# Chunked attention and token-mixing MLP in one kernel: holding back the input loads so that only about three are unfinished, with w_out in four transfers

## Chip, core, metric

The kernel runs on one core of one Trainium2 chip. The metric is the device time of one execution in microseconds (us), median of several runs. Most runs of a kernel agree closely, but some are slower whatever the kernel does; for this program on one core a run is called slow when it is over 1.5% above the fastest of its kernel.

## The reference

Inputs q, k and v are 8 batches x 8 heads x 576 positions x 64 in float32, 9.4 MB each. Attention works inside chunks of 64 positions; its output, regrouped to x of 8 x 576 x 512, goes through a mixing layer.

```python
# attention, per chunk of 64 positions
scores = scale * (q_c @ k_c.T);  attn = softmax(scores);  out = attn @ v_c
# mixing, per batch; x is the attention output, 576 x 512
wq, wk = x @ w_q, x @ w_k                 # 576 x 64 each
W_tok = scale_moe * wq @ wk.T
out = relu(W_tok @ x) @ w_out             # 576 x 512, float32
```

## The kernel before

All inputs of the core are 29.6 MB and the output is 9.4 MB. The loads convert float32 to float16 on the way, and are all issued by GpSimd, in program order. This is the part that the change touches (cuts are marked):

```python
def load_qk(b, part):               # q and k of batch b; part 0: 6 of 9 slices, part 1: 3
    a, e = TR[b][part]              # (in batch 0 it is 3 and 6)
    for src, dst in ((q, qn), (k, kn)):
        for u in range(2):          # two halves of the partitions
            nc.gpsimd.dma_start(dst[b][part][CH*u : CH*u+CH, 0 : e-a, :], src[b]. ...)

def load_v(b):                      # four loads of 144 KB (written)
    for n in range(0, NP, NP // 2):
        for u in range(2):
            nc.gpsimd.dma_start(vt[b % VB][...], v[b]. ...)

def load(b):
    load_qk(b, 0)
    load_v(b)
    if b == 1:
        nc.gpsimd.dma_start(wout[:], moe_w_out.rearrange("(i p) m -> p i m", p=P))
    load_qk(b, 1)
```

Loads of batches 0 to 3 are issued at the start; those of batch b+4 after the last attention unit of batch b, in program order. There are eight completion semaphores for these loads, used in turn, so that a load waits for the load eight before it: up to eight are unfinished at a time.

What uses the loads: VectorE transposes q and k of a batch as they come (`kT`, `qT`), TensorE forms the scores from them, and a fixed plan (`PLAN`) sets the order in which the units of several batches go to TensorE.

The softmax here doesn't subtract the row's maximum and nothing guards it: scores larger than these inputs give would overflow.

Of the kernel before, what the change touches and what calls it, by code (L numbers as in the profile page):

```python
# [34 lines left out]
def kernel(  # L35
# [10 lines left out]
    nc = tc.nc  # L46
    B, H, S, D = q.shape
    DM = moe_w_out.shape[0]
    DH = moe_w_q.shape[1]
    P = 128  # L50
# [6 lines left out]
    NI = DM // P  # L57
    HS = S // 2
    W = 2 * D + 2
    WS = 172  # L60
    VB = 4
    scale_attn = 1.0 / math.sqrt(D)
    scale_moe = 1.0 / math.sqrt(DH)
    TS = 3
# [6 lines left out]
    def each(n, shape, dt, name):  # L71
        return [sb.tile(shape, dt, name=f"{name}{i}") for i in range(n)]
# [8 lines left out]
    ]  # L81
    vt = each(VB, [P, NP, W], F16, "vt")
    wqk = sb.tile([P, NI, 2 * DH], F16, name="wqk")
    wout = sb.tile([P, NI, DM], F16, name="wout")
# [18 lines left out]

    of = out.rearrange("b s m -> (b s) m")

    def load_qk(b, part):
        a, e = TR[b][part]
        for src, dst in ((q, qn), (k, kn)):
            for u in range(2):
                nc.gpsimd.dma_start(  # L110
                    dst[b][part][CH * u : CH * u + CH, 0 : e - a, :],
                    src[b]
                    .rearrange("h s d -> (h s) d")
                    .rearrange("(u t p r) d -> u p t (r d)", u=2, t=NT, r=R)[u][:, a:e, :],
                )

    def load_v(b):
        for n in range(0, NP, NP // 2):
            for u in range(2):
                nc.gpsimd.dma_start(  # L120
                    vt[b % VB][CH * u : CH * u + CH, n : n + NP // 2, D * u : D * u + D],
                    v[b]
                    .rearrange("h s d -> (h s) d")
                    .rearrange("(u g p) d -> u p g d", u=2, p=CH)[u][:, n : n + NP // 2, :],
                )

    def clear_v(i, on_scalar):
        for h in range(2):
            o = vt[i][CH * h : CH * h + CH]
            z = D - D * h  # L130
            if on_scalar:
                nc.scalar.copy(
                    o.bitcast(F32)[:, :, z // 2 : z // 2 + D // 2],
                    zero.bitcast(F32)[CH * h : CH * h + CH, None, 0 : D // 2].broadcast_to(
                        [CH, NP, D // 2]
                    ),
                )
            else:
                nc.vector.memset(o[:, :, z : z + D], 0.0)
            nc.vector.memset(o[:, :, 2 * D + h], 1.0)  # L140
            nc.vector.memset(o[:, :, 2 * D + 1 - h], 0.0)

    def load(b):
        load_qk(b, 0)
        load_v(b)
        if b == 1:
            nc.gpsimd.dma_start(wout[:], moe_w_out.rearrange("(i p) m -> p i m", p=P))
        load_qk(b, 1)

    nc.vector.memset(zero[:], 0.0)  # L150
    for i in range(VB):
        clear_v(i, i > 1)
    load(0)
    make_identity(nc, ident[:])
    for w, o in ((moe_w_q, 0), (moe_w_k, DH)):
        nc.gpsimd.dma_start(wqk[:, :, o : o + DH], w.rearrange("(i p) j -> p i j", p=P))  # L156
    for b in range(1, VB):
        load(b)

# [57 lines left out]
    def attend(b, h, a):  # L217
        af = a.rearrange("p i c -> p (i c)")
        for c in range(2 * NJ):
            m = NCH * h + c  # L220
            if c < NCH:
                t, x = m // 4, m % 4
                lhsT = est[b % 2][t // TS][:, x // 2, 2 * (t % TS) + x % 2, :]
                rhs = vt[b % VB][:, m, :]
            else:
# [94 lines left out]
    def outp(a):  # L320
# [17 lines left out]
        held.append((of[n * P : n * P + P, :], os_))  # L338
        if done.get(B - 1 - VB) == 4:
            flush()  # L340
# [3 lines left out]
    def flush():  # L344
        if "gate" not in done:
            done["gate"] = 1
            nc.sync.dma_start(mark[:], kn[B - 1][1][0:1, 0, 0:2])
        for dst, src in held:
            nc.sync.dma_start(dst, src)
        held.clear()  # L350
# [4 lines left out]
    for u in PLAN.split():  # L355
        u, _, slot = u.partition(":")
        if u[0] == "T":
            tr(int(u[3]), u[1:3])
            continue
        a = ring[int(slot)]  # L360
        if u == "F":
            fill(a, 1)
        elif u == "O":
            outp(a)
        elif len(u) == 2:
            unit[u[0]](int(u[1]), a)
        else:
            b = int(u[2])
            unit[u[0]](b, int(u[1]), a)
            if u[0] == "A":  # L370
                done[b] = done.get(b, 0) + 1
                if done[b] == 4 and b + VB < B:
                    load(b + VB)
                    if b + VB == B - 1:
                        flush()
# [30 lines left out]
```

## Time and profile before

| | before |
|---|---|
| time, median of 3 runs (4 with the run beside the result: 126.16) | 126.52 us |
| span of the profiled run | 122.5 us |
| TensorE busy | 101.7 us (83%) |
| last load lands | 90.9 us |
| last TensorE instruction ends / last store packet | 118.7 / 121.0 us |

The landing of a load is the moment when the last of 16 DMA engines has raised the load's semaphore; I read it from the semaphore events of the trace, and where I quote landings of single loads, they come from there.

From the page of the kernel before: the busy tenths of TensorE and of the DMA engines in 40 slices of the span, what the DMA engines moved in each slice (bytes written), and the line of the queue that GpSimd issues to (packets, MB, time of its packets as a share of 16 engines' span).

```profile
PE   6912246497679996999999999999999999999970
DMA  1999999999999999999999999999938999994974
GB/s 10 125 142 176 183 195 168 168 200 191 176 164 168 174 160 177 199 162 176 179 176 155 191 184 159 189 191 164 168 48 314 361 375 366 383 386 146 335 277 165
q0 software_dynamic: 58416, 14.82, 128.0%
```

TensorE has holes up to slice 15 (counted from 0; it ends at 49 us) and is then full. Loads run at about 175 GB/s (written; twice that is read) until slice 28, then the stores, mostly at 310 to 386 GB/s. The queue's share is over 100% because several packets of one engine overlap.

Windows view of the kernel before: stretch, its length, then busy us and count for TensorE, its weight loads, VectorE, ScalarE and GpSimd, the granted TensorE clock, the DMA share and GB/s.

```profile
10.00:20.00 10.00, 4.60 (x182) 4.10 (x184) 5.92 (x9) 2.32 (x3) 9.93 (x15) 0.50 1.62 185
30.00:40.00 10.00, 7.39 (x226) 5.62 (x227) 8.41 (x14) 6.74 (x11) 8.26 (x13) 1.00 1.81 171
50.00:90.00 40.00, 39.87 (x856) 25.79 (x854) 34.30 (x54) 29.45 (x49) 31.24 (x44) 0.96 1.84 174
```

From 50 to 90 us TensorE is busy 39.87 of 40 us.

Timeline of VectorE in the kernel before (start, duration, instruction, idle time before it and what ended it):

```profile
13.13 0.98 DVE L179 STREAM_TRANSPOSE qT<-qn 128x768 f32<-128x768 f32 x1 [2.22 <-DMA qn<-in_q_dram]
18.02 0.98 DVE L179 STREAM_TRANSPOSE qT<-qn 128x768 f32<-128x768 f32 x1 [1.34 <-DMA qn<-in_q_dram]
94.42 0.57 DVE L179 STREAM_TRANSPOSE qT<-qn 128x384 f32<-128x384 f32 x1
```

The first two start 0.1 us after their load has landed (13.03, 17.93). The third, of the last batch, has no wait in front: its load had landed 4.6 us earlier, at 89.8 us. By then the loads lead.

The load issues, from the DMA view of the kernel before (KB are bytes written; the last number is the median time from issue to landing):

```profile
vt<-in_v_dram POOLq DMA_DIRECT2D x32, 144.0 KB, 6.4
qn<-in_q_dram POOLq DMA_DIRECT2D x16, 192.0 KB, 5.4
kn<-in_k_dram POOLq DMA_DIRECT2D x16, 192.0 KB, 5.7
qn<-in_q_dram POOLq DMA_DIRECT2D x16, 96.0 KB, 6.0
kn<-in_k_dram POOLq DMA_DIRECT2D x16, 96.0 KB, 5.6
```

A load takes 5.4 to 6.4 us, yet one of 192 KB lands every 1.0 us: most of its time it stands in the queue.

### The profile page before, as it was taken

What the parts mean: (1) busy time and instruction counts of PE and PEld (TensorE: products, weight loads), DVE (VectorE), ACT (ScalarE), POOL (GpSimd) and SP (SyncE); (2) the same over time, 40 slices, a digit from 0 to 9 for tenths busy, and PEclk for the clock granted to TensorE, in tenths of its full rate; (3) what the DMA queues carried; (4) which work ended last, traced back from release to release, by engine and by line L of the source; (5) the groups of instructions that cost most, each with busy time, mean ns of one, the idle gap of its engine ahead of it and who ended that gap; (6) DMA issues with size and microseconds to landing.
All of it is one profiled execution on the core that took longest, in us unless ns stands there. A gap on an engine that the chain in (4) does not pass through costs nothing.

```text
span 122.5 us, 4768 instructions
## 1 busy us (share of the span) xinstructions
PE 101.7 (83%) x2039; PEld 64.4 (53%) x2039; DVE 82.9 (68%) x146; ACT 76.4 (62%) x121; POOL 71.2 (58%) x105
## 2 busy tenths in 40 slices
PE   6912246497679996999999999999999999999970
PEld 2302145394566644375776575676649667543320
DVE  5765658738896994749997789997998987210000
ACT  7921122042459784558687878678786776899960
POOL 6999997348958985996995798789100000000000
PEclk9995555557999999589999999999999999999998
DMA  1999999999999999999999999999938999994974
GB/s 10 125 142 176 183 195 168 168 200 191 176 164 168 174 160 177 199 162 176 179 176 155 191 184 159 189 191 164 168 48 314 361 375 366 383 386 146 335 277 165
DMA packets 63626, 24.57 MB, mean 201 GB/s; under 512 B 40052, under 2 KB 58996, under 8 KB 63604
## 3 DMA queue, kind: packets, MB, share of 16 engines
q0 software_dynamic: 58416, 14.82, 128.0%
q1 hardware_dynamic: 5188, 9.44, 20.7%
q8 instruction: 16, 0.26, 0.9%
q14 instruction: 6, 0.05, 0.1%
HBM read 29.62 MB, written 9.44 MB: 319 GB/s over the span
## 4 chain that ended last, share of the span: by engine, by line
PE 59%; POOL 15%; DMA 14%; issue 4%; DVE 4%; ACT 2%; DVEq 0%; ACTq 0%; POOLq 0%
PE ring L325 26%; DMA wout<-in_moe_w_out_dram 8%; PE ring L203 7%; PE ring L228 7%; POOL vt L120 6%; PE ring L260 6%; DMA vt<-in_v_dram 5%; PE ring L250 5%; POOL kn L110 4%; PE ring L305 4%; POOL qn L110 3%; PE ring L291 3%; DVE xt L255 2%; POOL wqk L156 1%; PE ring L276 1%
## 5 line engine op out<-in xcount | busy, mean ns | idle before, releaser
L325 PE MATMUL ring<-wout,rmx 128*128 128x512 f16 x144 | 35.8, 387 | 0.1
L210 ACT ACTIVATE est<-ring 128x768 f16<-128x768 f32 x24 | 18.9, 810 | 22.1 <-PE ring L203 21.7
L203 PE MATMUL ring<-qT,kT 32*64 32x64 f16 x1152 | 16.9, 214 | 13.4 <-DVE kT L179 7.6
L120 POOL DMA_DIRECT2D vt<-in_v_dram x32 | 27.3, 876 | 0.8 <-PE ring L325 0.5
L238 DVE TENSOR_TENSOR xn<-ring,rec 128x640 f16<-128x640 f32 x32 | 26.4, 824 | 1.1
L110 POOL DMA_DIRECT2D qn<-in_q_dram x32 | 21.2, 677 | 8.4 <-DMA vt<-in_v_dram 7.6
L110 POOL DMA_DIRECT2D kn<-in_k_dram x32 | 20.7, 654 | 5.5 <-DMA vt<-in_v_dram 3.4
L203 PEld LDWEIGHTS <-kT 32*64 32x64 f16 x1152 | 14.1, 118 | 17.4 <-DVE kT L179 8.4
L313 ACT ACTIVATE rmx<-ring 128x576 f16<-128x576 f32 x32 | 19.3, 652 | 3.2 <-PE ring L305 3.0
L325 PEld LDWEIGHTS <-rmx 128*128 128x128 f16 x144 | 13.1, 99 | 14.3 <-issue 2.0
L179 DVE STREAM_TRANSPOSE kT<-kn 128x384 f32<-128x384 f32 (+1 forms) x16 | 19.5, 1221 | 0.6 <-DMA kn<-in_k_dram 0.4
L255 DVE COPY xt<-ring 128x1280 f16<-128x1280 f16 x16 | 12.9, 816 | 6.5 <-PE ring L250 5.4
L228 PE MATMUL ring<-vt,est 128*64 128x130 f16 x288 | 14.8, 240 | 1.2 <-ACT est L210 1.2
L179 DVE STREAM_TRANSPOSE qT<-qn 128x384 f32<-128x384 f32 (+1 forms) x16 | 12.2, 764 | 3.8 <-DMA qn<-in_q_dram 3.8
L228 PEld LDWEIGHTS <-est 128*64 128x64 f16 x288 | 11.1, 119 | 4.9 <-issue 1.9
L250 PE MATMUL ring<-ident,xn 128*128 128x128 f16 x160 | 12.7, 237 | 0.1
L250 PEld LDWEIGHTS <-xn 128*128 128x128 f16 x160 | 10.4, 107 | 2.5 <-issue 1.3
L337 ACT COPY qn<-ring 128x512 f32<-128x512 f32 x16 | 9.4, 588 | 3.3 <-PE ring L325 3.0
L337 ACT COPY kn<-ring 128x512 f32<-128x512 f32 x16 | 9.4, 589 | 2.0 <-PE ring L325 1.9
L237 DVE RECIPROCAL rec<-ring 128x10 f32<-128x10 f32 x32 | 6.6, 207 | 4.7 <-PE ring L228 4.6
L260 PE MATMUL ring<-xt,wqk 128*128 128x288 f16 x64 | 9.6, 295 | 0.1
L267 ACT CAST wT<-ring 128x576 f16<-128x576 f32 x8 | 5.1, 639 | 7.2 <-PE ring L260 7.2
(35 smaller groups left out, 86.2 us busy)
## 6 DMA issues: line engine op xcount, KB each, us to landing
vt<-in_v_dram POOLq DMA_DIRECT2D x32, 144.0 KB, 6.4
out_dram<-qn SPq DMA_DIRECT2D x16, 256.0 KB, 3.6
out_dram<-kn SPq DMA_DIRECT2D x16, 256.0 KB, 3.6
qn<-in_q_dram POOLq DMA_DIRECT2D x16, 192.0 KB, 5.4
kn<-in_k_dram POOLq DMA_DIRECT2D x16, 192.0 KB, 5.7
qn<-in_q_dram POOLq DMA_DIRECT2D x16, 96.0 KB, 6.0
kn<-in_k_dram POOLq DMA_DIRECT2D x16, 96.0 KB, 5.6
out_dram<-spare SPq DMA_DIRECT2D x4, 256.0 KB, 2.0
```

What stands on the lines that cost most here:

```text
L110: nc.gpsimd.dma_start(dst[b][part][CH * u : CH * u + CH, 0 : e - a, :], src[b] .rearrange("h s d -> (h s) d") .rearrange("(u t p r) d -> u ...
L120: nc.gpsimd.dma_start(vt[b % VB][CH * u : CH * u + CH, n : n + NP // 2, D * u : D * u + D], v[b] .rearrange("h s d -> (h s) d") .rearrange ...
L179: nc.vector.transpose(out=o, in_=src[b][part].bitcast(F32)[:, 0 : e - a, :].rearrange("p t (r d) -> p t r d", d=32),)
L203: nc.tensor.matmul(a[CH * u : CH * u + CH, i, o : o + CH], lhsT=k_of(b, TS * s + t, 2 * u + i, ch, e), rhs=q_of(b, TS * s + t, 2 * u + i, ...
L210: nc.scalar.activation(est[b % 2][s].rearrange("p i t c -> p i (t c)"), a[:, :, 0 : 2 * TS * CH], AF.Exp, scale=scale_attn,)
L228: nc.tensor.matmul(af[CH * (c % 2) : CH * (c % 2) + CH, o : o + W], lhsT=lhsT, rhs=rhs, start=True, stop=True,)
L238: nc.vector.tensor_tensor(out=xn[b % 2] .rearrange("p j (u h d) -> p j u h d", u=2, d=D)[:, :, :, h, :], in0=xv[:, :, 0 : 2 * D].rearrange ...
L250: nc.tensor.transpose(tx[:, i, j * P : j * P + P], xn[b % 2][:, j, (2 * i + n) * P : (2 * i + n) * P + P], ident[:],)
L260: nc.tensor.matmul(a[:, h, 0:HS], lhsT=wqk[:, i, :], rhs=xt[b % 2][i % 2][:, i // 2, h * HS : h * HS + HS], start=(i == 0), stop=(i == NI ...
L313: nc.scalar.activation(rmx[(b // 2) % 2].rearrange("p (h i) n -> p i h n", h=2)[:, i, :, o : o + HS], a[:, :, 0:HS], AF.Relu, scale=scale_moe,
L325: nc.tensor.matmul(a[:, 0, :], lhsT=rmx[pr % 2][:, i, tl * P : tl * P + P], rhs=wout[:, i, :], start=(i == 0), stop=(i == NI - 1),)
L337: nc.scalar.copy(os_, a[:, 0, :])
```

## The change

Its intent: keep only a short queue, so that loads are issued close to when they can run. Each load gets an estimated transfer time in us (1.0 for 192 KB of q or k and for a v load, 0.5 for 96 KB), and waits for the most recent earlier load that has more than 2.5 us of loads behind it, itself counted. For loads of 1.0 that is the third before it. w_out comes in four transfers.

```diff
+    AHEAD = 2.5
+    queue = []
+    def fetch(dst, src, us):
+        ins = nc.gpsimd.dma_start(dst, src).ins
+        ahead = 0.0
+        for name, u in reversed(queue):
+            if ahead + u > AHEAD:
+                tc.add_manual_dep(ins, name, ..., reason="pace")   # wait for its landing
+                break
+            ahead += u
+        queue.append((ins.name, us))
     # load_qk, load_v and the weights: nc.gpsimd.dma_start(...) -> fetch(..., us)
-            nc.gpsimd.dma_start(wout[:], moe_w_out.rearrange("(i p) m -> p i m", p=P))
+            for i in range(NI):
+                fetch(wout[:, i, :], moe_w_out[i * P : i * P + P, :], 0.7)
```

No instruction of TensorE, VectorE or ScalarE changes or moves.

More of the change, by code (lines that the diff above doesn't have):

```diff
@@ L104 @@
     of = out.rearrange("b s m -> (b s) m")
+    queue = []
[4 more added lines that the diff above has]
+            if ahead + u > AHEAD:
+                tc.add_manual_dep(
+                    ins,
+                    name,
+                    mybir.DependencyInfo(mybir.DependencyClass.Sync, mybir.DependencyReason.DATA),
+                    reason="pace",
+                )
+                break
+            ahead += u
+        queue.append((ins.name, us))
     def load_qk(b, part):
@@ L109, in load_qk @@
             for u in range(2):
-                nc.gpsimd.dma_start(
+                fetch(
                     dst[b][part][CH * u : CH * u + CH, 0 : e - a, :],
@@ L114, in load_qk @@
                     .rearrange("(u t p r) d -> u p t (r d)", u=2, t=NT, r=R)[u][:, a:e, :],
+                    (e - a) / 6,
                 )
@@ L119, in load_v @@
             for u in range(2):
-                nc.gpsimd.dma_start(
+                fetch(
                     vt[b % VB][CH * u : CH * u + CH, n : n + NP // 2, D * u : D * u + D],
@@ L124, in load_v @@
                     .rearrange("(u g p) d -> u p g d", u=2, p=CH)[u][:, n : n + NP // 2, :],
+                    1.0,
                 )
@@ L155 @@
     for w, o in ((moe_w_q, 0), (moe_w_k, DH)):
-        nc.gpsimd.dma_start(wqk[:, :, o : o + DH], w.rearrange("(i p) j -> p i j", p=P))
+        fetch(wqk[:, :, o : o + DH], w.rearrange("(i p) j -> p i j", p=P), 0.5)
     for b in range(1, VB):
```

## The prediction

> **What bounds the kernel now.** Span of the profile 122.5 us, timed median 126.52.
> (1) Until about 44 us the kernel follows its loads. In the timeline the VectorE transposes of q and k start 0.1 us after their load landed (Tk03 44.08 after 43.99). TensorE is busy 46%, 70% and 74% in 10-20, 20-30 and 30-40 us.
> (2) From about 50 to 100 us TensorE is full (99% and more, windows view), and the loads are ahead: the transposes start 3 to 5 us after landing; the last 4.6 (q) and 5.7 us (k).
> (3) The last load lands at 90.9 us; stores and the TensorE tail follow.
> The DMA engines limit the loads: one of 192 KB lands every 1.0 us, of 96 KB every 0.5 us, a v load of 144 KB every 1.1 us. Eight loads are unfinished at a time (eight semaphores in turn), so a load takes 5 to 6 us from issue to landing, mostly queued.
>
> **What the change does.** No compute instruction moves. GpSimd waits before nearly each load for one about three units back (about six for the small ones). w_out in four adds three issues of 0.75 us. Fewer unfinished loads can't bring an early load forward, since the queue drains nearly in order; they can only let it run dry.
>
> **Cost.** After a landing, GpSimd starts the waiting issue 0.28 us later (20.97 to 21.25), spends 0.65 us (q, k) or 0.87 us (v) on it, and the first packets come about 0.7 us after that (first load: issue ends 2.01, packets from 2.71). That is 1.6 to 1.9 us without new work, while two loads remain: at most 2.0 us, less 0.36 us between last packet and semaphore. So the slowest DMA engine is just not fed. The Trainium skill, page "DMA: Bandwidth & Descriptors", section "Anatomy of one DMA", puts the fixed part of a transfer at about 2.0 us; the trace agrees: 2.77 us for the first load, 0.5 us of it transfer.
> Second cost: every 5 to 6 us a 16 KB instruction fetch occupies a DMA engine for 0.9 to 1.4 us (queue 8). Today the other engines run ahead (the 16 parts of a load land up to 2.3 us apart), and the queue hides it. With three loads it can't: I expect each fetch to stop the stream for some 0.5 us.
> Estimate from a hand model of the queue with these durations: loads 4 to 7 us later at 44 us, the last one 8 to 18 us later (at 99 to 109 us).
>
> **How much counts.** The delay at 44 us is nearly all critical; later delays count beyond the 4.6 us lead. So 4 to 12 us; I take 5.5 us, below the middle, since a depth of 2.5 looks chosen by trial.
>
> **Predicted: 132.0 us, 8 in 10 between 126.0 and 140.0.** Faster by over 2%: 0.08. Within 2%: 0.25. Slower by over 2%: 0.67.
>
> **What would show it.** Last load landing at 97 us or later; median from issue to landing falling from 5.5-6.4 to about 3-4 us; DMA row with 7s and 8s instead of 9s before that; GpSimd's waits on DMA rising from 13 us to over 25; TensorE idle in 50-90 us; transposes 0.1 us behind landings after 50 us.
>
> **What would make it wrong.** Descriptors started before the issue ends (a gap under 1.6 us); or deep queues slowing the stream by themselves, for instance the slow engine catching up when the others idle; then it stays within 2%.

## More of the kernel before

The output tiles are held in the old q and k tiles and are stored only when the last load has landed:

```python
def flush():
    if "gate" not in done:
        done["gate"] = 1
        nc.sync.dma_start(mark[:], kn[B - 1][1][0:1, 0, 0:2])   # waits for the last load
    for dst, src in held:
        nc.sync.dma_start(dst, src)
    held.clear()
```

## The result

| | before | after |
|---|---|---|
| time, median of 4 runs | 126.16 us | 160.28 us |
| ratio of fast runs | | 1.282 (1.268 to 1.296) |
| span of the profiled run | 122.5 | 158.6 |
| last load lands | 90.9 | 129.1 |
| last TensorE instruction ends | 118.7 | 151.7 |
| last store packet | 121.0 | 157.2 |

A ratio is the mean time of one kernel's fast runs over that of the other's of the same rounds, so it is not quite the ratio of the medians. The kernel became 28% slower, far outside the predicted range.

The same lines of the changed kernel's page:

```profile
PE   6611261940578893969797692999393969999920
DMA  3999999999999899999999996999999939999994
GB/s 39 133 102 148 121 135 78 112 130 118 144 93 123 100 144 118 131 137 124 102 120 154 109 123 65 155 115 129 139 115 74 136 59 370 352 382 376 339 381 172
q0 software_dynamic: 58464, 14.82, 99.0%
```

TensorE now has holes to the end of the loads, in slice 32. The DMA row still shows mostly 9, but the bytes tell: 65 to 155 GB/s in place of 155 to 200 (from slice 3 on). The queue's share times the span is 0.99 x 158.6 = 157 us after and 1.28 x 122.5 = 157 us before: all packets together take as long as they did. The DMA engines are not slower, they have less to do at a time.

Windows view of the changed kernel:

```profile
10.00:20.00 10.00, 2.57 (x142) 2.20 (x146) 4.34 (x6) 1.03 (x2) 5.97 (x10) 0.58 1.31 134
30.00:40.00 10.00, 3.84 (x68) 3.09 (x70) 4.39 (x8) 1.27 (x2) 6.12 (x10) 0.67 0.96 118
50.00:90.00 40.00, 32.22 (x636) 20.04 (x633) 24.23 (x38) 24.16 (x40) 22.51 (x33) 0.96 1.28 126
```

From 50 to 90 us the load stream fell from 174 to 126 GB/s and TensorE from 39.9 to 32.2 us of work.

Timeline of VectorE in the changed kernel, late in the run:

```profile
101.64 0.98 DVE L200 STREAM_TRANSPOSE qT<-qn 128x768 f32<-128x768 f32 x1 [1.59 <-DMA qn<-in_q_dram]
113.20 0.85 DVE L200 STREAM_TRANSPOSE kT<-kn 128x384 f32<-128x384 f32 x1 [2.79 <-DMA kn<-in_k_dram]
```

These loads landed at 101.55 and 113.11 us: the transposes follow them by 0.1 us again, as 15 of the 22 after 50 us do. The lead of the loads is gone, and the whole kernel runs at the pace of its loads. The waits view of the changed kernel (engine, line, whom it waited for: us in total, times, longest) says the same for VectorE, and shows that GpSimd now stands still between issues:

```profile
DVE kT L200 <- DMA kn<-in_k_dram: 22.1, 13, 3.4
DVE qT L200 <- DMA qn<-in_q_dram: 22.0, 9, 4.4
POOL kn L110 <- DMA qn<-in_q_dram: 11.1, 8, 1.9
```

GpSimd's waits on DMA add up to 12.7 us before and about 42 us after. The load issues of the changed kernel:

```profile
vt<-in_v_dram POOLq DMA_DIRECT2D x32, 144.0 KB, 4.1
qn<-in_q_dram POOLq DMA_DIRECT2D x16, 192.0 KB, 3.9
kn<-in_k_dram POOLq DMA_DIRECT2D x16, 192.0 KB, 4.3
qn<-in_q_dram POOLq DMA_DIRECT2D x16, 96.0 KB, 3.7
kn<-in_k_dram POOLq DMA_DIRECT2D x16, 96.0 KB, 3.5
```

Each load is faster by itself, about 4 us in place of 6, and the stream of them is slower by 42% (129.1 over 90.9). How both can be true is what the experiments are about.

### The profile page after: what moved, and what is told of

It is laid out like the page before. It is cut to its first block, busy times and chain, and to the rows that moved or that the text cites. A ratio compares the mean times of both kernels' runs of the same rounds, so it can differ in the third digit from the quotient of the medians.

```text
span 158.6 us, 4786 instructions
## 1 busy us (share of the span) xinstructions
PE 106.4 (67%) x2039; PEld 67.5 (43%) x2039; DVE 82.3 (52%) x146; ACT 76.7 (48%) x121; POOL 72.6 (46%) x108
## 4 chain that ended last, share of the span: by engine, by line
DMA 55%; PE 20%; issue 9%; POOL 8%; DVE 3%; ACT 0%; DVEq 0%; POOLq 0%
DMA vt<-in_v_dram 25%; DMA qn<-in_q_dram 14%; DMA kn<-in_k_dram 13%; PE ring L346 12%; POOL vt L110 3%; POOL qn L110 3%; DMA wout<-in_moe_w_out_dram 3%; POOL kn L110 2%; PE ring L249 2%; PE ring L281 2%; DVE xt L276 2%; PE ring L312 1%; PE ring L326 1%; PE ring L224 1%; DVE xn L259 1%
## 5 line engine op out<-in xcount | busy, mean ns | idle before, releaser
L224 PEld LDWEIGHTS <-kT 32*64 32x64 f16 x1152 | 14.7, 124 | 37.5 <-DVE kT L200 15.8
L346 PEld LDWEIGHTS <-rmx 128*128 128x128 f16 x144 | 13.2, 100 | 16.5 <-issue 4.5
L249 PE MATMUL ring<-vt,est 128*64 128x130 f16 x288 | 15.9, 250 | 3.6 <-DVE xt L276 2.4
L249 PEld LDWEIGHTS <-est 128*64 128x64 f16 x288 | 12.0, 126 | 7.4 <-issue 4.8
L271 PE MATMUL ring<-ident,xn 128*128 128x128 f16 x160 | 13.7, 249 | 0.5 <-DVE xn L259 0.4
L271 PEld LDWEIGHTS <-xn 128*128 128x128 f16 x160 | 11.4, 113 | 2.7 <-issue 1.1
L281 PE MATMUL ring<-xt,wqk 128*128 128x288 f16 x64 | 10.1, 306 | 0.1
L312 PE MATMUL ring<-xn,wkn 128*64 128x256 f16 x80 | 6.4, 293 | 5.1 <-DVE wkn L304 5.1
```

Of the source, the lines that this page charges most:

```text
L224: nc.tensor.matmul(a[CH * u : CH * u + CH, i, o : o + CH], lhsT=k_of(b, TS * s + t, 2 * u + i, ch, e), rhs=q_of(b, TS * s + t, 2 * u + i, ...
L249: nc.tensor.matmul(af[CH * (c % 2) : CH * (c % 2) + CH, o : o + W], lhsT=lhsT, rhs=rhs, start=True, stop=True,)
L271: nc.tensor.transpose(tx[:, i, j * P : j * P + P], xn[b % 2][:, j, (2 * i + n) * P : (2 * i + n) * P + P], ident[:],)
L281: nc.tensor.matmul(a[:, h, 0:HS], lhsT=wqk[:, i, :], rhs=xt[b % 2][i % 2][:, i // 2, h * HS : h * HS + HS], start=(i == 0), stop=(i == NI ...
L346: nc.tensor.matmul(a[:, 0, :], lhsT=rmx[pr % 2][:, i, tl * P : tl * P + P], rhs=wout[:, i, :], start=(i == 0), stop=(i == NI - 1),)
```

## The experiments

The theory (A): a load has a round trip, from the landing that lets it go to its own landing, that is longer than the work which the few other loads leave, so the DMA engines run dry. Rivals: the four w_out transfers (B); deep queues disturb, so a short one should make loads fast (C); contention with compute or with instruction fetches (D, with E as its opposite); the added waits themselves (F); the number of loads rather than the amount of work (G).

### w_out in four, no pacing

```diff
-            nc.gpsimd.dma_start(wout[:], moe_w_out.rearrange("(i p) m -> p i m", p=P))
+            for i in range(NI):
+                nc.gpsimd.dma_start(wout[:, i, :], moe_w_out[i * P : i * P + P, :])
```

> The kernel before with w_out in four transfers and no pacing. Theory A (the pacing alone costs the time): the median within 1% of before, last load landing at 90 to 92 us. Rival B (the four w_out transfers and their extra issues delay what follows): some us slower, with the landings after w_out later by that much.

Measured: median 127.45 us (before beside it: 125.33), but three of four runs were slow ones. The fast one took 125.13 us, within the 123.87 to 125.69 us of the fast runs of before. The kernel was run again:

> The kernel before with w_out in four again, since three of its four runs were slow ones: within 1% of the kernel before in fast runs.

Measured: median 128.21 us (before: 125.80); again one fast run in six, 124.37 us, within 124.04 to 125.80. So fast runs agree with the kernel before. Even the medians of all runs differ by 2.1 and 2.4 us only, of the 34, so the pacing costs the rest. Both profiles fell in slow runs (last landings at 94.0 and 92.8 us, above the 90 to 92 expected). But the run without compute and without pacing, below, has w_out in four too and lands its last load at 90.7 us, as the kernel before does (90.9). Rival B falls.

### One load at a time

```diff
-    AHEAD = 2.5
+    AHEAD = 0.0
```

> The changed kernel with the pacing depth set from 2.5 to 0: each load waits for the one before it. It measures the whole round trip of one load: the time from landing to landing. Theory A (a round trip of fixed part plus transfer: 0.28 us wake, 0.65 or 0.85 us issue, 1.2 to 1.7 us until data flow, 0.36 us to the semaphore, and 0.5 or 1.0 us transfer): 192 KB loads every 3.7 to 4.0 us, 96 KB every 3.2 to 3.5, v every 3.8 to 4.2; last landing at 370 to 410 us. Rival C (loads slow down only because deep queues of the other engines disturb them): periods near 2.5 us and the last landing near 250 us.

Measured, in one run: 386.18 us, last landing at 356.9. The DMA view of this run:

```profile
vt<-in_v_dram POOLq DMA_DIRECT2D x32, 144.0 KB, 3.5
qn<-in_q_dram POOLq DMA_DIRECT2D x16, 192.0 KB, 3.5
kn<-in_k_dram POOLq DMA_DIRECT2D x16, 192.0 KB, 3.5
qn<-in_q_dram POOLq DMA_DIRECT2D x16, 96.0 KB, 2.6
```

The queue is empty whenever a load is issued here, so these times contain no queueing: 3.5 us of the 3.9 to 4.3 us under pacing are there with nobody in front. From the events of the trace, means over each kind, in us:

| load | landing to issue | issue | to the first packet | first of 16 parts lands | last part lands | landing to landing | in the full queue of before |
|---|---|---|---|---|---|---|---|
| 96 KB q, k | 0.28 | 0.63 | 0.70 | 1.63 | 1.98 | 2.89 | 0.5 |
| 192 KB q, k | 0.35 | 0.66 | 0.70 | 2.35 | 2.81 | 3.82 | 1.0 |
| 144 KB v | 0.37 | 0.84 | 0.70 | 2.16 | 2.65 | 3.86 | 1.1 |

(The three columns after the issue count from its end.) A line through the q and k loads, 2.89 and 3.82 us, gives 1.96 us fixed and 0.93 us per 96 KB. The page "DMA: Bandwidth & Descriptors" of the Trainium skill, section "Anatomy of one DMA — SWDGE (gpsimd) path", gives about 2.0 us for the fixed part, and this is near it: 1.96 us with the 0.28 us of waking in it, 1.68 without. The slope does not agree with the full queue: there 96 KB cost 0.5 us.

A load that meets an empty queue moves its bytes at about half the rate of the stream on average. The packets of the 32 lone 192 KB loads show when: 11 to 17 start per tenth of a us for the first 0.8 us, then up to 38, the rate of the full stream. Single packets take as long as before (median 60 ns for those of 512 bytes in both runs), so it is fewer at a time. Why the start is slow these runs do not show. The same page, section "Measured (HBM→SBUF, 128 partitions, SWDGE, issued from GpSimd)", lists 138 GB/s for 64 KB and 341 GB/s for 1 MB, the same tendency (for 128 partitions; the loads here write 64); here 192 KB in the 1.56 us from the first packet (0.70) to the landing of the median part (2.62) less 0.36 us for the semaphore are some 126 GB/s, written.

Theory C falls: a lone load is no faster. Its transfer is slower. The expectation of theory A held for 192 KB and for v (3.82 and 3.86 us), but not for 96 KB (2.89 in place of 3.2 to 3.5) nor for the last landing (356.9 in place of 370 to 410): the fixed part is smaller, and the part that goes with the bytes larger, than in that sum.

### The loads without compute

The matmuls, transposes and evictions are cut, and the stores write what was loaded, so the result is wrong:

```diff
-    for u in PLAN.split():
-        ...
+    for b in range(VB, B):
+        load(b)
+    ...                      # spare tiles, and slices that no load writes, set to zero
+    for n in range(4 * NCH):
+        ...; held.append((of[n * P : n * P + P, :], os_))
+    flush()
```

> The changed kernel's loads, pacing 2.5, with all matmuls, transposes and evictions left out and the stores writing what was loaded (a wrong result on purpose). No TensorE program, so no instruction fetches in the DMA queues and no work of VectorE next to GpSimd. Theory A (round trip of a load longer than the work that two others leave): the last load still lands late, at 112 to 120 us, some 10 us of the 38 being fetches. Rival D (contention with the compute engines or fetches): the last load lands at 90 to 97 us. Rival E (round trip alone, fetches cost nothing): at 127 to 130 us.

> The same loads without compute and without pacing, w_out in four: the control of the run before. All theories: last landing at 86 to 90 us; about 2 us less than with compute if the fetches cost the slowest DMA engine what it lags behind, 2 us.

Measured, one run each, of unknown state: last landing at 125.9 us paced and 90.7 us with the pacing depth at 1000, which paces nothing. The rows of the paced run's page, then of the free one's:

```profile
DMA  2999999999899979999999999999989949999994
GB/s 34 131 97 144 122 140 107 115 124 134 103 128 111 135 91 126 104 135 124 119 124 148 108 106 121 146 119 120 131 113 110 116 54 376 382 383 380 381 382 164
q0 software_dynamic: 58464, 14.82, 102.2%
```

```profile
DMA  0999999999999999999999999999991999999992
GB/s 7 126 136 169 183 185 174 160 192 181 156 141 175 195 172 160 192 171 150 181 195 166 164 193 180 160 190 189 157 157 34 382 383 378 384 384 378 383 382 102
q0 software_dynamic: 58464, 14.82, 131.5%
```

With no matmul, transpose or eviction on the core, pacing costs 35.2 of the 38.2 us that the last landing moves in the full kernel. Rival D falls, and so does a part of my own sum: in these runs there is no packet in queue 8, that of the instruction fetches (the full kernel has 16), and the paced stream gained 3.2 us, not the 10 that I expected of it. So 125.9 is nearer to E (127 to 130) than to my own 112 to 120. The free run's expectation missed too: it lands with compute and without it at the same time (90.9, 90.7), so the fetches cost the unpaced stream nothing.

The packets of the paced run show how the queue runs dry. Count of data packets in tenths of a us, read from the trace (38 per tenth is the full rate of q and k):

```
us      55.1 55.3 55.5 55.7 55.9 ... 56.5 56.8 57.0 57.2 57.4 57.5 57.7 57.9 58.1
packets   39   33   23    9    3        2   11   17   11    0    0   23   37   38
k load issued at 55.47 to 56.13 (it waited for a landing at 55.19)
```

For 1.8 us (55.8 to 57.6) the engines start about a seventh of the packets of the full rate. From 55.9 to 56.7 only 2 to 3 packets a tenth are left, the rate of one engine of 16; and of the k load issued at 52.29 us, 15 parts have landed by 56.22 and the last lands at 57.23. The waiting load's first packets come 0.7 us after its issue has ended (56.8), and the full rate another 1.1 us later (57.9). The 16 parts of a load land 0.3 to 2.2 us apart here, without any instruction fetch. What makes single engines late after a restart these runs do not show.

### The depth

```diff
-    AHEAD = 2.5
+    AHEAD = 3.5        # and 4.5, and 6.0 in two other kernels
```

> The changed kernel with the pacing depth raised from 2.5 to 3.5, about four loads unfinished. Theory A, revised by the round trip that was measured one load at a time (3.8 us for a load of 1 us of transfer, so about 4.4 us of work must be unfinished): still short, last load landing at 96 to 108 us, time 128 to 138 us. Rival F (the waits themselves, one more semaphore wait before nearly every issue, cost the time, at any depth): last landing above 120 us, time above 150 us.

> Pacing depth 4.5, about five loads unfinished. Theory A: nearly enough, last landing at 91 to 98 us, time within 0 to 4 us of the kernel before. Rival F: above 150 us as at any depth.

> Pacing depth 6.0: about as many loads unfinished as the eight semaphores leave anyway (5.9 us of work on average before). Theory A: last landing at 91 to 94 us, time within 1.5% of the kernel before. Rival F (the waits themselves cost): still 5% or more slower.

Measured, with the runs above in one table. "Unfinished" is the mean amount of unfinished work, in the change's own transfer estimates (83.8 us for all loads), from the start of the span to the last landing; "mean time" is the mean time of that work from issue to landing, unfinished work times last landing over 83.8.

| depth | unfinished, us | mean time, us | last landing, us | time, us (median) |
|---|---|---|---|---|
| 0 | 0.77 | 3.3 | 356.9 | 386.18 |
| 2.5 (the change) | 2.62 | 4.0 | 129.1 | 160.28 |
| 3.5 | 3.43 | 4.6 | 111.7 | 142.06, ratio 1.134 (1.122 to 1.147) |
| 4.5 | 4.28 | 5.2 | 101.9 | 133.58, ratio 1.064 (1.054 to 1.073) |
| 6.0 | 5.37 | 5.9 | 92.0 (in a slow run) | 127.49; its one fast run 125.47 |
| none (before) | 5.63 | 6.1 | 90.9 | 126.16 |

Rival F falls: at depth 6.0 82 of the 102 loads wait for an earlier one, as 82 do under the change and 87 of 99 before, by the semaphores in the traces; and its one fast run lies within the fast runs of before beside it (124.04 to 125.80). So pacing hardly adds waits, it makes them wait for a nearer load. Each step of depth gives time back, until the queue is about as deep as the eight semaphores make it (5.37 against 5.63 us). My numbers for 3.5 and 4.5 were too good (landing at 96 to 108 and 91 to 98 us were expected): the 4.4 us of work that I had worked out from the lone round trip is too little. With 4.28 us the stream still lost 11 us; 5.37 us was enough, in a slow run.

The table also splits the loss, by arithmetic on means and not by an experiment. With 2.62 us of work unfinished and the mean time of a lone load, 3.3 us, the loads would take 83.8 x 3.28 / 2.62 = 105 us, 14 us over the kernel before. The other 24 us come from the mean time growing to 4.0 us although the queue runs dry: a load waits behind the two others, and for the last of 16 engines that finish at different times. The traces divide this second part (means weighted by the same estimates): the first of a load's 16 parts lands 2.31 us after the end of its issue in place of the 2.12 of a lone load, and the last part 1.00 us after the first in place of 0.44. So of the growth of 0.76 us some 0.2 comes before the first part lands, and 0.56, about three quarters, is engines that finish apart. Why they do stays open.

### Three larger loads

From the second batch on q and k come in two loads of 288 KB each and v in two of 288 KB, and each load waits for the third before it:

```diff
-            if ahead + u > AHEAD:  ...
+        if len(queue) >= 3:
+            tc.add_manual_dep(ins, queue[-3][0], ..., reason="pace")
     # one q tile and one k tile per batch with 10 slices; a load takes all 9
```

> Still three loads unfinished at a time, but each load larger: from the second batch on q and k in two loads of 288 KB (1.5 us of transfer) and v in two of 288 KB (2 us), half as many loads. Theory A (what counts is the work that is unfinished, against a round trip of 3.8 us that grows only by the transfer): the last load lands at 94 to 112 us, time 126 to 142 us. Rival G (the number of unfinished loads counts, the chip needs many to be fast): last landing at 125 us or later as with the change.

Measured: 147.01 us in the fast run of two, last landing at 118.8. Between both expectations: larger loads win back 10 of 38 us with no more loads unfinished (2.7 on average from 20 us on, 3.2 under the change), so the number alone (G) is not it. The landing is above theory A's 94 to 112 us, and the time above its 126 to 142. But on average 4.4 us of work are unfinished from 20 us on (2.7 loads), about as in the run of depth 4.5 (4.5 us from 20 us on, 5.2 loads), which lands at 101.9. A load counts as unfinished as a whole until its last part has landed, and with few large ones more of that is probably done already (not measured); the parts of a load land 0.2 to 3.4 us apart here. Work unfinished is the better measure but not a sufficient one; in this one comparison, more and smaller loads kept the engines fed better than few large ones at the same amount. Why by so much stays open.

### Pacing only some batches

```diff
+    paced = {"on": True}
-            if ahead + u > AHEAD:
+            if paced["on"] and ahead + u > AHEAD:
     def load(b):
+        paced["on"] = b < 2      # the other kernel: b > 5
```

> The changed kernel, depth 2.5, with pacing for the loads of batches 0 and 1 only. Theory A: these land as late as with the full change (k of batch 1 at 38 to 39 us, 8.8 us later than before), nothing is made up afterwards since the DMA engines have no spare rate, the last load lands at 98 to 101 us, and the time grows by 6 to 9 us. If the stage to 44 us had slack (the run with the later v halves hints at some after 34 us), by 4 to 6 us.

> Pacing, depth 2.5, for the loads of batches 6 and 7 only. Theory A: last load landing about 10 us later (100 to 102 us); the lead of 4 to 5 us absorbs the first part, TensorE ends 4 to 6 us later; the stores, which start after the last load, start 10 us later and may end last; the time grows by 5 to 9 us. If the lead absorbed all of it: under 2 us.

Measured: ratio 1.086 (1.073 to 1.099) with the first two batches paced, 1.087 (1.077 to 1.097) with the last two, about 10.8 us each (two and four fast runs; the record calls both unclear). Both are above what I expected. Whether a delay in the first loads counts as a whole is not shown: the profile of that kernel fell in a slow run, so its landings can't be set against the kernel before. In the last two batches the landing moved by 13.2 us (104.0), the last TensorE instruction by 9.6 us (128.4) and the last store packet by 10.9 us (132.0). So the lead of the loads was worth 3.6 us to TensorE, near the 4.6 that the trace of before shows, but less for the kernel as a whole, since the stores start with the last landing.

### Later halves of v, unpaced

An attempt at a faster kernel, from the kernel before: the second half of each v moves behind the next batch's first q and k.

```diff
         load_qk(b, 0)
-        load_v(b)
+        if b > 1:
+            load_v(b - 1, (1,))
+        load_v(b, (0, 1) if b in (0, B - 1) else (0,))
```

> The kernel before, unpaced, with the second half of each v (batch 1 on) loaded one batch later, behind the next batch's first q, k and in front of its first v half. It takes 2 us of transfers out of the way of the loads on which the stage to 44 us waits. If that stage is bound by bytes, as theory A has it, the transposes there start 2 us earlier from batch 2 on and the time falls by 1 to 2 us (about 1%); if it is bound by the work on the engines, no change.

Measured: ratio 0.995 (0.985 to 1.004), the same. The transposes of batch 2 came 0.7 us (q) and 0.9 us (k) earlier (31.28 and 33.28 us), not the 2 us expected, and those of batch 3 not at all (43.68 and 44.58 us against 43.17 and 44.08 before), with no idle time of VectorE in front. So from about 34 us on the kernel before is not held by its loads alone. No version that beats the kernel before was found.

## Why the prediction was wrong

The direction, slower, and the mechanism, a queue that runs dry, were right. The size was not: 5.5 us were predicted and 34 measured. Point by point:

- "DMA engines limit the loads", "mostly queued": right. The packets took 157 us of the 16 engines before and after; the loads only kernel without pacing ends its loads at the same 90.7 us.
- "1.6 to 1.9 us without new work, while two loads remain", "just not fed": this is the step that failed. The parts were each read correctly (0.28 us wake, 0.65 us issue, 0.70 us to the first packet, 0.36 us semaphore), but the first packet is not the full rate. I added a transfer at the rate of the full stream (1.0 us for 192 KB) where a load into an empty queue takes 1.86 us more than its fixed 1.96; the round trip came out as 3.0 us and measured 3.82. By the split above this mis-sized term is some 14 of the 38 us. And two loads leave 2.0 us of work only if all 16 engines hold equal shares of it: in the changed kernel the parts of a load land 0.3 to 3.0 us apart, 1.0 on average, and by the same split about three quarters of the other 24 us go with that. "4 to 7 us later at 44 us" measured 16 us for the load of that moment (k of batch 3 at 60.5 in place of 44.0), and "8 to 18 us later" for the last one 38.2 us.
- "Each fetch to stop the stream for some 0.5 us": wrong. Without these fetches and without compute the paced loads end only 3.2 us earlier. (And the parts of a load land up to 2.9 us apart before, not 2.3.)
- "Later delays count beyond the 4.6 us lead": nearly right for TensorE, which ended 33.0 us later for a landing 38.2 us later. I left out the stores. They take 28.5 us after the last landing with nothing else on the core (119.2 - 90.7), and before, the span ended 31.6 us after it (122.5 - 90.9). So of any delay of the last load at most about 3 us can be hidden, whatever TensorE's lead. Measured: 38.2 us of delay, 36.1 us of longer span.
- "I take 5.5 us, since a depth of 2.5 looks chosen by trial": a guess about the author in place of the model's own middle, 8 us. The model was too small by itself; this made it worse.
- Signs: last landing after 97 us (129.1), time from issue to landing of 3 to 4 us (3.5 to 4.3), GpSimd's waits over 25 us (42), TensorE idle in 50 to 90 us (7.8 us), transposes 0.1 us behind landings (15 of 22), nearly all as said. The DMA row with 7s and 8s did not come: its share exceeds 1 (1.84 before, 1.28 after), and a digit stops at 9.

## What to carry to other kernels

A transfer that takes 6 us from issue to landing is not slow if one lands every us: here queueing is what kept the engines fed, and shortening the queue is free only down to the round trip times the rate. Measure that round trip with one load at a time on the chip, rather than adding it up from first packets and stream rates, and leave well over it, since a load lands with the slowest of its engines (here 2.9 to 3.9 us alone, while 4.3 us of unfinished work was too little and 5.4 enough). In a kernel that waits for bytes, a wait in front of a load costs once it lets the queue run dry, and a lead of the loads late in the kernel hides less than it seems when other transfers are held until the last load has landed.

## What the Trainium skill lacked or had wrong

- "DMA: Bandwidth & Descriptors", section on the anatomy of a SWDGE transfer: it calls the cost of descriptor generation small and variable. Here each load held GpSimd for 0.54 us (128 KB of w_out) to 0.88 us (144 KB of v), and that time is in series with the wait when loads are paced. How much of it is descriptor generation the trace does not tell.
- The same section says that the wait for a semaphore happens on the issuing sequencer before dispatch. The trace agrees, and adds what it costs: 0.28 us from a landing to the start of the next issue, 0.53 us in 7 of the 8 lone loads that wait for two semaphores.
- The same page has no figure for how much must be unfinished to keep the engines full. Here 2.6, 3.4, 4.3 and 5.4 us of stream work gave last landings at 129, 112, 102 and 92 us (the last in a slow run).
- The same page's table of sizes has lower rates for smaller transfers, but no page sets a lone load against a full queue. Here a load that met an empty queue needed 0.93 us per 96 KB against 0.5 in the stream, and, at 192 KB, was slow in the first 0.8 us of its packets.
